# State-space layer with a gated feed-forward block on one core: the first token block's normalization, its high and low halves, the first feed-forward products, and the stores at the end

## The chip, the cores and the metric

The kernel runs on one NeuronCore of a Trainium2 chip, as one program. The metric is the device time of one execution in microseconds (us), the median of the runs; lower is better. Engines are named as in the profile: PE is TensorE (matmuls; PEld its weight loads), DVE is VectorE, ACT is ScalarE, POOL is GpSimd and SP is SyncE, which here only issues DMAs.

## What is computed

The input is 2048 tokens of 640 channels, in float32. The reference, cut to what matters:

```python
mod = (silu(c) @ w_mod)                      # six rows: sa, ca, ga, sb, cb, gb
h = layernorm(x) * (1 + ca) + sa
x = x + ga * (causal_conv(h, K) + h * D_skip)   # K: length 2048, from 128 complex states per channel
h = layernorm(x) * (1 + cb) + sb
x = x + gb * ((silu(h @ w1) * (h @ w3)) @ w2)   # w1, w3: 640 x 1728, w2: 1728 x 640
```

The convolution goes by a long transform in the reference; the kernel makes the same transform out of matmuls. The change touches none of that stage but one instruction of its layer norm. It touches the second half: the second layer norm, the gated feed-forward layer (FFN), and the final output.

## The kernel before

**Front.** Up to about 352 us of the profile the kernel makes the convolution's filters, the first layer norm, the transforms and the products in the frequency domain. These tasks are placed by a planner from a fixed list. At the end of it the inverse transform gives the convolved rows back, 128 tokens by 640 channels at a time ("slots"; 16 slots, four to a block of 512 tokens; blocks b = 0 to 3). The last 128 columns of block 0's four slots come last: `inverse_load` fetches the rows (tile `low`) and `inverse` multiplies them into PSUM tiles `iy` (lines 1234 and 1236). The inverse of the other three blocks is spread in pieces between the FFN's tiles of blocks 0 and 1.

**Second layer norm, block 0** (`ln2`, line 645, with `ln_norm`, 629, and `rsqrt`, 246). DVE sums the statistics, and `rsqrt` makes 1/sqrt(variance) for 4 values a partition with 13 small DVE instructions, each of which needs the one before: a start value from the bits of the float (a shift and a multiply-add on integers), three Newton steps of three instructions, and one for the shift -mean/sqrt(variance). Then the four slots are normalized into `xn` (slots 0 and 2 on ACT, 1 and 3 on DVE), turned by PE into PSUM banks `tp00` to `tp04` (one for each 128 channels k, 512 tokens wide; tags acc0 to acc4, which the FFN later sums in), scaled and shifted into `v` (even k on DVE, odd k on ACT), rounded by ACT into the high half `xh`, and the rest is subtracted out as the low half `xl` (even k on DVE, odd k on POOL; `split`, 625). While PE has nothing to do, `awake` gives it products that nobody reads.

**FFN** (`ffn`, 764). The hidden width of 1728 is 13 f-tiles of 128 and an odd one of 64, number 13, whose two 64-wide halves (w1 and w3) share a tile. The order is 0, 13, 1, 2, ... 12. `up` (1043) sums for an f-tile two PSUM tiles `gu` (w1 and w3; the odd tile one) over k = 0 to 4, with three matmuls for each k: wh times xh, wh times xl, wl times xh, where wh and wl are the high and low halves of the weights. The `gu` tiles have three PSUM banks. For block 0 the first two f-tiles' three sums are made together: 45 matmuls. `gate` (1056) makes `th` on ACT, then `a` on DVE in two steps, and its halves; `down` (1080) multiplies by w2 into `acc0` to `acc4`. Blocks 2 and 3 go by a scheme that shares products between the pair (`pair_up`, `pair_down`).

**End.** For block 3 the last f-tile is 12, and the one before is 11. `acc0` to `acc3` hold the output of the four slots for channels 0 to 511; `acc4` holds channels 512 to 639 turned, so `turn_last` (1896) copies it out on ACT (`oc`) and turns it by PE into `to`. `output` (1090) adds the residual `x` on DVE and stores two slots at once, 160 KB for each of four groups of 32 partitions. SP and ACT issue these stores in turn.

**What sets the order.** A scheduler places the instructions of the second half by priority; where the code uses `Engines`, `InOrder` (138, 156) or `order`, the written order is kept. Every DMA that SP or ACT issues takes the next of eight semaphores in turn (DMAHW0 to DMAHW7), and waits, before it is issued, until the DMA that used that semaphore before has landed. An engine does its instructions strictly in order, DMA issues among them.

Of the kernel before, what the change touches and what calls it, by code (L numbers as in the profile page):

```python
# [210 lines left out]
class K:  # L211
# [34 lines left out]
    def rsqrt(self, pool, var, n, tag, mean, scale=1.0, work=None):  # L246
# [347 lines left out]
    def inverse(self, j0, nj, z, ps, tag, bufs, d0, d1, part=None):  # L594
# [4 lines left out]
        for o, n in cuts if part is None else cuts[part:part + 1]:  # L599
            for j in range(0, nj, 2):  # L600
                py = [ps.tile([P, 512], F32, name=f"iy{j0 + j + p}_{d0 + o}", tag=tag, bufs=bufs) if ps else self.pbank(f"iy{j0 + j + p}") for p in range(2)]
                for p in range(2):
                    for q in range(4):
                        r, c = 64 * ((q + p) % 2), 32 * q
                        mm = nc.tensor.matmul(py[p][c:c + 32, :n], self.wd[r:r + 64, j0 + j + p, q // 2],
                                              z[q // 2][r:r + 64, j + p, o:o + n], start=True, stop=True, tile_position=(r, c))
# [22 lines left out]
    def ln_norm(self, b, pool, stats=None):  # L629
# [8 lines left out]
        for j in range(4):  # L638
            if j % 2:
                nc.vector.tensor_scalar(xn[:, j, :], xs[:, j, :], rstd[:, j:j + 1], nb[:, j:j + 1], op0=ALU.mult, op1=ALU.add)  # L640
            else:
                nc.scalar.activation(xn[:, j, :], xs[:, j, :], AF.Identity, scale=rstd[:, j:j + 1], bias=nb[:, j:j + 1])
        return xn

    def ln2(self, b, pool, ps, stats=None, po=None):
# [5 lines left out]
        xl = to.tile([P, KT, 512], F32R, name=f"xl{b}", tag="xl", bufs=1)  # L651
        for k in range(KT):
            if po:
                pt = po.tile([P, 512], F32, name=f"tp{b}{k}", tag=f"acc{k}")
            else:
                pt = ps.tile([P, 512], F32, name=f"tp{b}{k}", tag="gu", bufs=3)
            for j in range(4):
                nc.tensor.transpose(pt[:, j * P:(j + 1) * P], xn[:, j, k * P:(k + 1) * P], self.ident)
            v = pool.tile([P, 512], F32, name=f"v{b}{k}", tag="v", bufs=4)
            if po and k % 2:  # L660
                nc.scalar.activation(v, pt, AF.Identity, scale=self.cols[:, 1, k:k + 1], bias=self.cols[:, 0, k:k + 1])
            else:
                nc.vector.tensor_scalar(v, pt, self.cols[:, 1, k:k + 1], self.cols[:, 0, k:k + 1], op0=ALU.mult, op1=ALU.add)
            self.split(xh[:, k, :], xl[:, k, :], v, nc.gpsimd if po and k % 2 else nc.vector)
# [283 lines left out]
    def pair_down(self, wp, pool, ps, po):  # L948
# [20 lines left out]
        for b in (2, 3):  # L969
            acc = None  # L970
            for m in order:
# [14 lines left out]
                if pend is not None:  # L986
                    self.down(*pend, *([(4, 0, 1, 2)] if end else []))
# [55 lines left out]
    def up(self, b, tiles, xh, xl, ps):  # L1043
# [4 lines left out]
        for ks in [(k,) for k in range(KT)] if len(tiles) > 1 else [range(KT)]:  # L1048
            for pg, wh, wl in every:
                for k in ks:  # L1050
                    nc.tensor.matmul(pg, wh[:, k, :], xh[:, k, :], start=(k == 0), stop=False)  # L1051
                    nc.tensor.matmul(pg, wh[:, k, :], xl[:, k, :], start=False, stop=False)  # L1052
                    nc.tensor.matmul(pg, wl[:, k, :], xh[:, k, :], start=False, stop=(k == KT - 1))  # L1053
# [62 lines left out]
    def run(self):  # L1116
# [119 lines left out]
        self.hold = nc.tensor.prev = self.inverse(0, 4, z, ps, "gu", 3, cut, D)  # L1236
# [719 lines left out]
```

## Time and profile before

| what | value |
|---|---|
| runs | 931.13, 931.5, 933.71 us; median 931.5 us |
| profiled execution, own time | 932.87 us |
| its span in the trace | 931.1 us, so 1.77 us lie around the span |
| mean granted TensorE clock | 0.984 |
| DVE, ACT, POOL busy | 74%, 56%, 38% of the span |
| block 0, from the last inverse rows to the FFN | 352 to 375 us |
| FFN of all blocks | 365 to 924 us |

The profile's page gives the busy time of each engine, and the chain of work that ended last. The views used below are the waits of one engine (who it waited for, how long), the timeline of a window (start, length, engine, line, what is written and read, and in brackets the idle time before it and who ended it), the windows (busy time of each engine in a stretch), and the DMAs of a window (size, and microseconds from issue to landing). "x5" is the number of instructions joined in a row, and the length is then that of all of them.

### The profile page before, as it was taken

To read this page: it belongs to the slowest core of one execution; us is meant where nothing else is said; L and a number is where in the kernel's file an instruction comes from. 1 tells how busy PE (TensorE), PEld (TensorE's weight loads), DVE (VectorE), ACT (ScalarE), POOL (GpSimd) and SP (SyncE) were. 2 spreads that over 40 slices of the span, in tenths; PEclk is the share of its full clock that TensorE was granted. 3 is DMA by queue.
4 is the path that set the end of the run, shared out by engine and by line. 5 is a ranking of instruction groups with operands and counts; after the bars stand their busy time and mean duration, and the time that the engine had idled before them with its cause. 6 is when DMAs were issued, how large, how long until landed. Compare 5 with 4: busy or idle time off the path is not lost.

```text
span 931.1 us, 22000 instructions
## 1 busy us (share of the span) xinstructions
PE 846.5 (91%) x8983; PEld 678.7 (73%) x8983; DVE 692.1 (74%) x1213; ACT 519.2 (56%) x889; POOL 354.2 (38%) x341
## 2 busy tenths in 40 slices
PE   1367888999989997999999999999999999999997
PEld 1155767778868754777877788888888888888885
DVE  7999999999989776656765756476567777765653
ACT  5989999999877733423423334344333444445331
POOL 1589989899998461000000000001133332101640
PEclk9978999999999998999999999999999999999999
DMA  8965574332242568975455362232232111123242
GB/s 194 305 223 148 174 188 107 94 110 78 70 126 80 145 170 208 218 195 149 117 128 127 92 178 85 84 87 84 71 85 57 56 56 39 35 84 114 85 142 57
DMA packets 124556, 112.77 MB, mean 121 GB/s; under 512 B 11944, under 2 KB 106664, under 8 KB 123176
## 3 DMA queue, kind: packets, MB, share of 16 engines
q1 hardware_dynamic: 123720, 110.46, 43.6%
q8 instruction: 70, 1.15, 0.5%
q10 hardware_dynamic: 736, 0.92, 0.4%
q14 instruction: 30, 0.25, 0.1%
HBM read 90.38 MB, written 20.97 MB: 120 GB/s over the span
## 4 chain that ended last, share of the span: by engine, by line
PE 71%; DVE 11%; ACT 8%; DMA 4%; issue 3%; SPq 1%; POOL 0%; DVEq 0%; ACTq 0%; POOLq 0%
PE acc L1088 20%; PE p L837 17%; PE gu L1051 7%; PE gu L1053 7%; PE gu L1052 7%; PE ps L147 3%; DVE yy L147 3%; PE kps L147 2%; PE fh L147 2%; PE fz L147 2%; ACT tr L147 2%; PE fk L147 1%; DVE fp L147 1%; DVE xx L147 1%; DMA xs<-in_x 1%
## 5 line engine op out<-in xcount | busy, mean ns | idle before, releaser
L1051 PE MATMUL gu<-xh,wh 128*128 128x512 f32 x270 | 106.1, 398 | 1.6 <-ACT xh L626 1.4
L1053 PE MATMUL gu<-xh,wl 128*128 128x512 f32 x270 | 105.4, 390 | 0.0
L1052 PE MATMUL gu<-xl,wh 128*128 128x512 f32 x270 | 105.1, 389 | 0.0
L147 ACT ACTIVATE tr<-ph 128x512 f32<-128x512 int32 (+1 forms) x160 | 93.6, 602 | 8.9 <-POOL ph L147 3.0
L856 POOL TENSOR_TENSOR ws<-wp 128x256 f32<-128x256 f32 x13 | 9.6, 741 | 230.9 <-DVE x L627 116.0
L147 POOL TENSOR_TENSOR ph<-p,p 128x1024 int32<-128x1024 int32 x40 | 79.1, 1978 | 5.9 <-ACT tr L147 4.9
L147 DVE TENSOR_TENSOR yy<-yy,tr 128x512 f32<-128x512 f32 (+1 forms) x80 | 75.4, 943 | 1.4 <-POOL yy L147 1.2
L740 ACT ACTIVATE wh<-wr 128x640 fp32r<-128x640 f32 x51 | 34.9, 731 | 61.8 <-PE gu L1052 61.1
L837 PE MATMUL p<-x,wch 128*128 128x512 f32 x208 | 68.3, 389 | 0.0
L1051 PEld LDWEIGHTS gu<-xh,wh 128*128 128x128 f32 x270 | 50.6, 188 | 17.6 <-DVE al L627 2.1
L147 POOL TENSOR_TENSOR yy<-e,e 128x512 f32<-128x512 f32 x48 | 51.6, 1087 | 23.4 <-ACT e L147 19.7
L753 POOL MEMSET w2l<- 64x640 f32 x1 | 0.6, 632 | 157.0 <-PE acc L1088 157.0
L147 PE MATMUL kps<-yy,xx 128*32 128x64 f32 x2560 | 49.0, 227 | 11.5 <-DVE xx L147 9.1
L1053 PEld LDWEIGHTS gu<-xh,wl 128*128 128x128 f32 x270 | 50.7, 188 | 11.2 <-DVE wl L750 0.4
L1052 PEld LDWEIGHTS gu<-xl,wh 128*128 128x128 f32 x270 | 50.7, 188 | 10.2 <-DVE xl L627 0.2
L147 DVE TENSOR_TENSOR xx<-tr,xx 128x512 f32<-128x512 f32 x80 | 54.2, 680 | 2.2 <-ACT tr L147 1.7
L874 DVE TENSOR_TENSOR s<-p,s 128x512 f32<-128x512 f32 x52 | 34.7, 682 | 26.8 <-ACT s L872 22.8
L1064 ACT ACTIVATE th<-gu 128x512 f32<-128x512 f32 x26 | 15.5, 598 | 68.1 <-PE gu L1053 68.1
L1066 DVE TENSOR_TENSOR a<-a,gu 128x512 f32<-128x512 f32 x26 | 17.8, 686 | 46.6 <-PE gu L1053 46.4
L147 PEld LDWEIGHTS kps<-yy,xx 128*32 128x32 f32 x2560 | 43.2, 113 | 12.3 <-POOL yy L147 4.7
L147 PE MATMUL ps<-wk,xb 128*64 128x128 f32 x640 | 47.6, 295 | 2.9 <-issue 1.2
L147 PE MATMUL fh<-sp,wb 128*64 128x128 f32 x640 | 43.9, 280 | 5.7 <-issue 2.3
(381 smaller groups left out, 2386.5 us busy)
## 6 DMA issues: line engine op xcount, KB each, us to landing
wr<-in_w SPq DMA_DIRECT2D x52, 320.0 KB, 3.7
zd<-zt SPq DMA_DIRECT2D x39, 256.0 KB, 3.6
w2r<-in_w SPq DMA_DIRECT2D x26, 320.0 KB, 2.9
wp<-in_w SPq DMA_DIRECT2D x26, 320.0 KB, 3.2
wq<-in_w SPq DMA_DIRECT2D x26, 320.0 KB, 3.1
low<-zd SPq DMA_DIRECT2D x24, 320.0 KB, 6.3
xs<-in_x SPq DMA_DIRECT2D x16, 320.0 KB, 11.9
hs<-hb SPq DMA_DIRECT2D x20, 256.0 KB, 3.7
```

What stands on the lines that cost most here:

```text
L147: self.prev = self.k.order(f(*a, **kw), self.prev)
L740: self.nc.scalar.activation(wh[:, i], raw[:, i], AF.Copy)
L753: self.nc.gpsimd.memset(w2l[64:].bitcast(F32), 0.0)
L837: nc.tensor.matmul(to, t[:, o], y[:, k], start=start and k == i == 0, stop=stop and (k, i) == (n - 1, 2), skip_group_check=True)
L856: G.tensor_tensor(s[0], a21, a22, op=ALU.add)
L874: add = lambda o, bk, s: V.tensor_tensor(o, bk, s, op=ALU.add)
L1051: nc.tensor.matmul(pg, wh[:, k, :], xh[:, k, :], start=(k == 0), stop=False)
L1052: nc.tensor.matmul(pg, wh[:, k, :], xl[:, k, :], start=False, stop=False)
L1053: nc.tensor.matmul(pg, wl[:, k, :], xh[:, k, :], start=False, stop=(k == KT - 1))
L1064: nc.scalar.activation(th, gu[0], AF.Tanh, scale=0.5)
L1066: nc.vector.tensor_mul(a, a, gu[1])
L1088: nc.tensor.matmul(acc[k], *two(a, w), start=(m == 0 and i == 0), stop=(m == 12 and i == 2))
```

## The change

Six edits, all in the second half but for one instruction:

1. `rsqrt`: the two integer instructions become one (a multiply by -0.5 and an add). Where no work tile is given (all second layer norms), three Newton steps are replaced by one step of third order and one Newton step: 10 DVE instructions where there were 13. The first layer norm has a work tile, and loses one instruction.
2. `inverse` of block 0's last columns: PSUM tiles acc0 to acc3 instead of the three `gu` banks.
3. `ln_norm`, block 0: slot 2 is shared, columns 0 to 383 on ACT and 384 to 639 on DVE.
4. `ln2`, block 0: the turns stand in a fixed order, all four slots of a k together, slots 1, 0, 3, 2. `xh` is made by ACT straight from PSUM. Then `v` and `xl` for k = 0, 1, 2, 4 are made on DVE in turn, each k complete before the next; for k = 3 `v` on ACT after the last `xh`, and `xl` on POOL.
5. `up`, block 0, first two f-tiles: the two sums of f-tile 0 first, with the xl products of a k one step later than its other products, then the odd tile's 15 matmuls. 45 matmuls as before.
6. End: the three matmuls of f-tile 11 into acc2 stand behind `turn_last`; the residual is added for acc0, acc1, the last 128 channels (all four slots at once), acc2, acc3 in turn, and each of the five is stored by itself in four DMAs of 64 KB: 20 DMAs where there were 8 of 160 KB.

```diff
@@ rsqrt
-        nc.vector.tensor_scalar(wi, v.bitcast(I32), 1, None, op0=ALU.logical_shift_right)
-        nc.vector.tensor_scalar(wi, wi, -1.0, float(0x5F3759DF), op0=ALU.mult, op1=ALU.add)
-        for i in range(3):
...
+        nc.vector.tensor_scalar(wi, v.bitcast(I32), -0.5, float(0x5F3759DF), op0=ALU.mult, op1=ALU.add)
+        if work:
...
+        else:
+            nc.vector.tensor_mul(t, w, w)
+            nc.vector.tensor_mul(t, t, v)
+            nc.vector.scalar_tensor_tensor(t, t, -10.0 / 3.0, t, op0=ALU.add, op1=ALU.mult)
+            nc.vector.scalar_tensor_tensor(w, t, 5.0, w, op0=ALU.add, op1=ALU.mult)
+            nc.vector.tensor_mul(t, w, w)
+            nc.vector.scalar_tensor_tensor(t, t, -0.5 * 0.375 ** 3, v, op0=ALU.mult, op1=ALU.mult)
+            nc.vector.scalar_tensor_tensor(y, t, 1.5 * 0.375, w, op0=ALU.add, op1=ALU.mult)
@@ ln_norm
+            if stats and j == 2:
+                shared = 384
+                nc.scalar.activation(xn[:, j, :shared], xs[:, j, :shared], AF.Identity, scale=rstd[:, j:j + 1], bias=nb[:, j:j + 1])
...
+        if stats:
+            nc.vector.tensor_scalar(xn[:, 2, shared:], xs[:, 2, shared:], rstd[:, 2:3], nb[:, 2:3], op0=ALU.mult, op1=ALU.add)
@@ ln2
+            if po:
+                for j in (1, 0, 3, 2):
+                    last = self.order(nc.tensor.transpose(pt[:, j * P:(j + 1) * P], xn[:, j, k * P:(k + 1) * P], self.ident), last)
+                high.append(nc.scalar.activation(xh[:, k, :], pt, AF.Identity, scale=self.cols[:, 1, k:k + 1], bias=self.cols[:, 0, k:k + 1]))
+                todo.append((v, pt, k))
+                continue
...
+        for v, pt, k in todo:
+            scale, shift = self.cols[:, 1, k:k + 1], self.cols[:, 0, k:k + 1]
+            if k == 3:
+                self.order(nc.scalar.activation(v, pt, AF.Identity, scale=scale, bias=shift), high[-1])
+            else:
+                before = self.order(nc.vector.tensor_scalar(v, pt, scale, shift, op0=ALU.mult, op1=ALU.add), before)
+            i = (nc.gpsimd if k == 3 else nc.vector).tensor_tensor(xl[:, k, :], v, xh[:, k, :].bitcast(F32), op=ALU.subtract)
+            before = before if k == 3 else self.order(i, before)
@@ end of pair_down
-                    self.down(*pend, *([(4, 0, 1, 2)] if end else []))
+                    self.down(*pend, *([(4, 0, 1)] if end else []))
...
-        self.down(*pend, (2,))
-        self.down(*prev, (3,))
-        self.down(*pend, (3,))
-        self.output(3, acc, ps, pt)
+        for k in (2, 3):
+            self.down(*prev, (k,))
+            self.down(*pend, (k,))
+        x = self.x2[3]
+
+        def store(j, s):
+            for q in range(4):
+                (nc.scalar if q % 2 else nc.sync).dma_start(self.ov[q, :, 12 + j.start:12 + j.stop, s], x[q * 32:(q + 1) * 32, j, s])
+        for j in range(4):
+            nc.vector.tensor_add(x[:, j, :512], acc[j], x[:, j, :512])
+            store(slice(j, j + 1), slice(0, 512))
+            if j == 1:
+                nc.vector.tensor_add(x[:, :, 512:], pt, x[:, :, 512:])
+                store(slice(0, 4), slice(512, D))
@@ up
+            for k in range(KT + 1):
+                for w, x, c in ((1, xh, k), (2, xh, k), (1, xl, k - 1)):
+                    for t in every[:2] if 0 <= c < KT else ():
+                        last = self.order(nc.tensor.matmul(t[0], t[w][:, c, :], x[:, c, :], start=(c == 0 and w == 1 and x is xh), stop=(x is xl and c == KT - 1)), last)
+            every = every[2:]
...
@@ run
-        self.hold = nc.tensor.prev = self.inverse(0, 4, z, ps, "gu", 3, cut, D)
+        self.hold = nc.tensor.prev = self.inverse(0, 4, z, po, "acc", 0, cut, D)
```

The order of the built program at three places. A row names the line, the operation, the tile written, the tiles read and the shape; "waits" names the engines or DMA semaphores that the instruction waits for. First PE in block 0, from the turns to the first sums (gu0_00 and gu0_01 are f-tile 0's two sums, gu0_130 the odd tile's), before:

```order
L658 MATMUL tp00_5618<-ident_58,xn0_5611 128x128 x2
L658 MATMUL tp01_5627<-ident_58,xn0_5611 128x128 x2
...
L658 MATMUL tp04_5654<-ident_58,xn0_5611 128x128 x2
L1051 MATMUL gu0_00_5667<-xh0_5616,wh0_0_5413 128x512
L1051 MATMUL gu0_01_5668<-xh0_5616,wh0_0_5413 128x512
L1051 MATMUL gu0_130_5669<-xh0_5616,wh0_13_5495 128x512
L1052 MATMUL gu0_00_5667<-xl0_5617,wh0_0_5413 128x512
L1053 MATMUL gu0_00_5667<-xh0_5616,wl0_0_5440 128x512
```

and of the changed kernel:

```order
L674 MATMUL tp00_5615<-ident_58,xn0_5607 128x128 x4
L674 MATMUL tp01_5622<-ident_58,xn0_5607 128x128 x4
...
L674 MATMUL tp04_5643<-ident_58,xn0_5607 128x128 x4
L1089 MATMUL gu0_00_5664<-xh0_5613,wh0_0_5412 128x512
L1089 MATMUL gu0_01_5665<-xh0_5613,wh0_0_5412 128x512
L1089 MATMUL gu0_00_5664<-xh0_5613,wl0_0_5439 128x512
L1089 MATMUL gu0_01_5665<-xh0_5613,wl0_0_5439 128x512
...
L1089 MATMUL gu0_00_5664<-xl0_5614,wh0_0_5412 128x512
L1089 MATMUL gu0_01_5665<-xl0_5614,wh0_0_5412 128x512
```

Before, PE made two slots' turns for all five k and then the other two slots', and the first xl product was the fourth product. Now a k is turned completely before the next, the first xl product is the ninth, and the odd tile's products stand behind all 30 of f-tile 0. Next DVE at the same place, before:

```order
L640 TENSOR_SCALAR xn0_5611<-x_low_4178,rs_y_n0_5595,rs_n_n0_5596 128x640
L663 TENSOR_SCALAR v00_5623<-tp00_5618,cols_67 128x512 [waits PE_49]
L663 TENSOR_SCALAR v02_5641<-tp02_5636,cols_67 128x512 [waits PE_49]
L627 TENSOR_TENSOR xl0_5617<-v00_5623,xh0_5616 128x512 [waits Activation_49]
L663 TENSOR_SCALAR v04_5659<-tp04_5654,cols_67 128x512 [waits DVE_49,PE_49]
L627 TENSOR_TENSOR xl0_5617<-v02_5641,xh0_5616 128x512 [waits Activation_49]
L627 TENSOR_TENSOR xl0_5617<-v04_5659,xh0_5616 128x512 [waits Activation_49]
```

and of the changed kernel:

```order
L650 TENSOR_SCALAR xn0_5607<-x_low_4177,rs_y_n0_5594,rs_n_n0_5595 128x640
L654 TENSOR_SCALAR xn0_5607<-x_low_4177,rs_y_n0_5594,rs_n_n0_5595 128x256
L687 TENSOR_SCALAR v00_5616<-tp00_5615,cols_67 128x512 [waits Activation_49]
L688 TENSOR_TENSOR xl0_5614<-v00_5616,xh0_5613 128x512 [waits DVE_49]
L687 TENSOR_SCALAR v01_5623<-tp01_5622,cols_67 128x512 [waits Activation_49]
L688 TENSOR_TENSOR xl0_5614<-v01_5623,xh0_5613 128x512 [waits DVE_49]
L687 TENSOR_SCALAR v02_5630<-tp02_5629,cols_67 128x512 [waits Activation_49]
L688 TENSOR_TENSOR xl0_5614<-v02_5630,xh0_5613 128x512 [waits DVE_49]
```

Before, a `v` on DVE waited for PE's turns, and ACT's `xh` read it. Now `v` waits for ACT, which reads the same bank for `xh` first, and nothing but `xl` reads it. Last, the stores on SP at the end of the program (ACT issues as many, in turn with SP), before, behind the last weight loads:

```order
L963 DMA wq1_9440<-in_w2 128x640 [waits DMAHW3_49,DVE_49]
L147 DMA out_0<-x23_5544 32x1280 [waits DMAHW5_49,DVE_49]
L147 DMA out_0<-x23_5544 32x1280 [waits DMAHW6_49]
L147 DMA out_0<-x23_5544 32x1280 [waits DMAHW1_49,DVE_49]
L147 DMA out_0<-x23_5544 32x1280 [waits DMAHW2_49]
```

and of the changed kernel:

```order
L988 DMA wq1_9428<-in_w2 128x640 [waits DMAHW3_49,DVE_49]
L147 DMA out_0<-x23_5543 32x512 [waits DMAHW5_49,DVE_49]
L147 DMA out_0<-x23_5543 32x512 [waits DMAHW6_49]
L147 DMA out_0<-x23_5543 32x512 [waits DMAHW0_49,DVE_49]
L147 DMA out_0<-x23_5543 32x512 [waits DMAHW2_49]
L147 DMA out_0<-x23_5543 32x4x128 [waits DMAHW4_49,DVE_49]
L147 DMA out_0<-x23_5543 32x4x128 [waits DMAHW6_49]
L147 DMA out_0<-x23_5543 32x512 [waits DMAHW0_49,DVE_49]
L147 DMA out_0<-x23_5543 32x512 [waits DMAHW2_49]
L147 DMA out_0<-x23_5543 32x512 [waits DMAHW4_49,DVE_49]
L147 DMA out_0<-x23_5543 32x512 [waits DMAHW6_49]
```

With 8 stores each had a semaphore of its own, so what its first wait names is an older DMA. With 20 stores the third set of four (the last 128 channels, 32x4x128) takes the semaphores of the first set (acc0), the fourth (acc2) those of the second (acc1), and the fifth (acc3) those of the third.

One more place differs: on SP the load of w2's rows for f-tile 2 moves behind the next eight loads of `x` and four of `low`. The other differences of the order are a row or two wide.

More of the change, by code (lines that the diff above doesn't have):

```diff
@@ L254, in rsqrt @@
         wi = w.bitcast(I32)
-        nc.vector.tensor_scalar(wi, v.bitcast(I32), 1, None, op0=ALU.logical_shift_right)
-        nc.vector.tensor_scalar(wi, wi, -1.0, float(0x5F3759DF), op0=ALU.mult, op1=ALU.add)
-        for i in range(3):
-            if work:
+        nc.vector.tensor_scalar(wi, v.bitcast(I32), -0.5, float(0x5F3759DF), op0=ALU.mult, op1=ALU.add)
+        if work:
+            for i in range(3):
                 nc.vector.tensor_copy(u, w)
-            nc.vector.tensor_mul(t, u, w)
-            nc.vector.scalar_tensor_tensor(t, t, -0.5, v, op0=ALU.mult, op1=ALU.mult)
-            nc.vector.scalar_tensor_tensor(y if i == 2 else w, t, 1.5, w, op0=ALU.add, op1=ALU.mult)
+                nc.vector.tensor_mul(t, u, w)
+                nc.vector.scalar_tensor_tensor(t, t, -0.5, v, op0=ALU.mult, op1=ALU.mult)
+                nc.vector.scalar_tensor_tensor(y if i == 2 else w, t, 1.5, w, op0=ALU.add, op1=ALU.mult)
+        else:
[6 more added lines that the diff above has]
+            nc.vector.scalar_tensor_tensor(y, t, 1.5 * 0.375, w, op0=ALU.add, op1=ALU.mult)
         m, s = mean
@@ L600, in inverse @@
             for j in range(0, nj, 2):
-                py = [ps.tile([P, 512], F32, name=f"iy{j0 + j + p}_{d0 + o}", tag=tag, bufs=bufs) if ps else self.pbank(f"iy{j0 + j + p}") for p in range(2)]
+                py = [ps.tile([P, 512], F32, name=f"iy{j0 + j + p}_{d0 + o}", **(dict(tag=tag, bufs=bufs) if bufs else dict(tag=f"{tag}{j + p}"))) if ps else self.pbank(f"iy{j0 + j + p}") for p in range(2)]
                 for p in range(2):
@@ L638, in ln_norm @@
         for j in range(4):
-            if j % 2:
+            if stats and j == 2:
+                shared = 384
+                nc.scalar.activation(xn[:, j, :shared], xs[:, j, :shared], AF.Identity, scale=rstd[:, j:j + 1], bias=nb[:, j:j + 1])
+            elif j % 2:
                 nc.vector.tensor_scalar(xn[:, j, :], xs[:, j, :], rstd[:, j:j + 1], nb[:, j:j + 1], op0=ALU.mult, op1=ALU.add)
@@ L651, in ln2 @@
         xl = to.tile([P, KT, 512], F32R, name=f"xl{b}", tag="xl", bufs=1)
+        last = before = None
+        todo, high = [], []
         for k in range(KT):
@@ L1047, in up @@
         every = [(pg, wh[:, i], wl[:, i]) for (m, wh, wl), g in zip(tiles, gu) for i, pg in enumerate(g)]
[L1048 to L1053, printed above, removed]
+        last = None
+        if len(tiles) > 1:
+            for k in range(KT + 1):
[3 more added lines that the diff above has]
+            every = every[2:]
+        for pg, wh, wl in every:
+            for k in range(KT):
+                for w, x in ((wh, xh), (wh, xl), (wl, xh)):
+                    mm = nc.tensor.matmul(pg, w[:, k, :], x[:, k, :], start=(k == 0 and x is xh and w is wh), stop=(k == KT - 1 and w is wl))
+                    if len(tiles) > 1:
+                        last = self.order(mm, last)
         return gu
```

8 lines of the change are left out of this document (3 added, 5 removed).

## The prediction

> **What bounds the kernel now.** I read the page first, for the share of the chain of work that ended last, then PE's waits, then the two places of the change in the timeline, then the DMAs of the end.
>
> ```profile
> span 931.1 us, 22000 instructions
> PE 71%; DVE 11%; ACT 8%; DMA 4%; issue 3%; SPq 1%; POOL 0%; DVEq 0%; ACTq 0%; POOLq 0%
> ```
>
> The chain lies on PE for 71%. How firmly, the windows say (length, then PE, PEld, DVE, ACT, POOL busy, granted clock, DMA share, GB/s): two in the FFN, and two at block 0's start.
>
> ```profile
> 358.00:360.00 2.00, 2.00 (x4) 0.57 (x2) 1.61 (x10) 0.00 (x0) 0.00 (x0) 0.69 1.01 315
> 360.00:362.00 2.00, 1.23 (x10) 1.01 (x10) 1.13 (x2) 1.73 (x2) 0.00 (x0) 1.00 1.03 309
> 450.00:500.00 50.00, 49.92 (x271) 39.63 (x270) 32.91 (x72) 18.16 (x29) 0.00 (x0) 1.00 0.45 113
> 660.00:720.00 60.00, 60.00 (x267) 49.26 (x266) 42.58 (x60) 22.20 (x35) 17.81 (x20) 1.00 0.29 77
> ```
>
> From 375 to 925 us, PE's list of waits has one row:
>
> ```profile
> PE gu L1051 <- DVE a L1065: 0.2, 1, 0.2
> ```
>
> So between block 0's first products and the end PE is a solid row of matmuls. Time taken out ahead of it moves the whole row forward; time taken from other engines inside it (the shorter root of blocks 1 to 3 among it) is worth nothing. Only two places can gain: the hole before the first products, and the end, where PE is done and the stores land.
>
> **Block 0.** The timeline from the root to the next f-tile (start, length, engine, line, tiles):
>
> ```profile
> 356.59 3.63 PE L147 MATMUL awake<-x_low,ident 128*128 128x512 f32 x5
> 357.38 0.17 DVE L253 TENSOR_SCALAR rs_v_n<-mv_n 128x4 f32<-128x4 f32 x1
> 359.76 0.16 DVE L265 SCALAR_TENSOR_TENSOR rs_n_n<-mv_n,rs_y_n 128x4 f32<-128x4 f32 x1
> 360.01 1.73 ACT L642 ACTIVATE xn<-x_low,rs_n_n,rs_y_n 128x640 f32<-128x640 f32 x2 [12.94 <-DVE rs_n_n L265]
> 360.03 1.13 DVE L640 TENSOR_SCALAR xn<-x_low,rs_y_n,rs_n_n 128x640 f32<-128x640 f32 x2
> 360.99 2.40 PE L658 MATMUL tp<-ident,xn 128*128 128x128 f32 x20 [0.77 <-ACT xn L642]
> 362.56 1.53 DVE L663 TENSOR_SCALAR v<-tp,cols 128x512 f32<-128x512 f32 x2 [1.40 <-PE tp L658]
> 362.77 1.45 ACT L661 ACTIVATE v<-tp,cols 128x512 f32<-128x512 f32 x2 [1.03 <-PE tp L658]
> 364.12 2.93 ACT L626 ACTIVATE xh<-v 128x512 fp32r<-128x512 f32 x5
> 364.79 0.97 PE L1051 MATMUL gu<-xh,wh 128*128 128x512 f32 x3 [1.40 <-ACT xh L626]
> 365.40 3.00 POOL L627 TENSOR_TENSOR xl<-v,xh 128x512 fp32r<-128x512 f32 x2 [15.03 <-ACT xh L626]
> 373.14 0.39 PE L1051 MATMUL gu<-xh,wh 128*128 128x512 f32 x1
> 374.95 0.39 PE L1053 MATMUL gu<-xh,wl 128*128 128x512 f32 x1
> 374.01 0.60 ACT L1064 ACTIVATE th<-gu 128x512 f32<-128x512 f32 x1 [5.67 <-PE gu L1053]
> 375.55 0.47 PE L1051 MATMUL gu<-xh,wh 128*128 128x512 f32 x1 [0.21 <-DVE a L1065]
> 376.53 0.40 PE L1051 MATMUL gu<-xh,wh 128*128 128x512 f32 x1
> ```
>
> *Root.* From the first of 13 instructions (357.38) to the last (359.76) are 12 steps in 2.38 us, 0.198 each; three fewer are 0.6 us. ACT's first `xn` starts at 359.4 instead of 360.01. The awake products end at 360.22 (356.59 + 3.63), before the first turn, which needs an `xn` of 0.87 (half of 1.73) and so comes at 360.3. The clock is granted in full from 360 on in the second window, so the earlier turns meet it.
>
> *To the first product.* Before, 4.78 us pass from ACT's first `xn` to the product at 364.79: both slots on ACT, turns, `v`, `xh`. After, the slot that ends last is slot 2: ACT needs 0.87 and then 384 columns, an estimate of 0.6 (`th`, 512 columns, took 0.60; a 640-column `xn` 0.87), so 1.45 us; DVE has its 256 columns by then too (1.13 for two slots, 0.3 more). Of the 20 turns three stand before slot 2's first; 17 follow at 0.11 to 0.12 (2.40 for 20), 1.9 us. With 0.07 for the handover the first product starts 3.42 us after ACT's first `xn`. `xh` of k = 0 is no later: its turns end at 1.8, and an eviction by ACT takes 0.7 to 0.8 (1.45 for two), so 2.6. First product: 359.41 + 3.42 = **362.8, 2.0 us earlier**.
>
> *The 45 products.* Eight steps from 373.14 to 374.95 are 0.226 us each; 45 are 10.2, and before they took 375.55 - 364.79 = 10.76, the rest being starts of k that waited. After, f-tile 0's sums are complete at product 30, so `th`, `a` and the next weights' halves have the odd tile's 3.4 us to be made in, and the next f-tile starts without a wait at 373.0. Its first three products also run at 0.68 rather than 0.98 (375.55 to 376.53). Gains 0.5 and 0.3. Sum of block 0: **2.8**.
>
> *What it costs.* `v` on DVE now queues behind ACT's `xh`, and each pair of `v` and `xl` is a DVE chain; a late `xl` holds PE's row. DVE needs 0.8 for `v` (1.53 for two), and for `xl`:
>
> ```profile
> L627 DVE TENSOR_TENSOR xl<-v,xh x13: 677/684/1771, 364.8 to 572.5; 128x512 fp32r<-128x512 f32 x13
> ```
>
> 0.69, but 1.77 at worst, which in this block fell while POOL made its two `xl`. Counted from ACT's first `xn`: `xl` of k = 0, 1, 2, 4 at 4.2, 5.8, 7.3, 8.9; PE wants them at 5.2, 6.6, 8.0, 9.8 (products 9, 15, 21 and 29). POOL's one `xl` of 1.5 (3.00 for two) starts behind ACT's sixth eviction at about 6.2 and is done at 7.8, wanted at 9.3. It meets DVE's third `xl`; a stretch by 1.1 makes a stall of 0.4, a full block of 1.5 one of 0.85. I take 0.2: **block 0 gains 2.6**, with ends 1.6 (0.85 of stall, 0.2 for a slower 384-column piece, 0.15 for handovers) and 3.0 (PSUM banks for all four slots spare the statistics a wait).
>
> The Trainium skill, page "SBUF — State Buffer", section "SBUF: two separate sides", says that a DVE instruction with two SBUF inputs and a GpSimd instruction that reads SBUF lock each other out for a whole instruction. The 1.77 beside 0.68 agrees with it; by that rule the stall is the 0.85 above if POOL comes first, and the whole change is worth 0.65 less.
>
> Behind it, the shift must not run into data. PE's next rows of the inverse need `low`, loaded late because each DMA waits for the landing of the one eight issues before it:
>
> ```profile
> 365.85 4.96 SPq L589 DMA_DIRECT2D low<-zd  x4
> x<-in_x SPq DMA_DIRECT2D x1, 320.0 KB, 7.4
> low<-zd SPq DMA_DIRECT2D x4, 320.0 KB, 11.7
> L605 PE MATMUL iy<-low,x_low x16: 429/441/453, 386.2 to 389.7; 64*32 64x320 f32 x16
> ```
>
> The x load of 358.43 landed after 7.4, at 365.83, and only then `low` was issued; the last of the four (370.3) landed at about 382, and its reader ran at 386.2. Moved forward 2.6 it runs at 383.6: 1.5 us are left, and `low` gets a 320 KB load less ahead of it.
>
> **First layer norm.** One instruction less:
>
> ```profile
> 57.07 0.23 DVE L147 TENSOR_SCALAR rs_w_h<-rs_w_h 128x16 int32<-128x16 int32 x1
> ```
>
> DVE is full there; I take 0.1, between 0 and 0.25.
>
> **The end.**
>
> ```profile
> 920.99 1.38 DVE L147 TENSOR_TENSOR x<-acc,x 128x512 f32<-128x512 f32 x2 [2.15 <-PE acc L147]
> 924.20 0.69 DVE L147 TENSOR_TENSOR x<-acc,x 128x512 f32<-128x512 f32 x1 [0.70 <-PE acc L147]
> 924.80 0.41 DVE L147 TENSOR_TENSOR x<-to,x 128x256 f32<-128x256 f32 x1
> 925.25 0.87 ACTq L147 DMA_DIRECT2D out<-x  x2
> out<-x ACTq DMA_DIRECT2D x1, 160.0 KB, 3.0
> out<-x ACTq DMA_DIRECT2D x2, 160.0 KB, 4.0
> sp<-in_x SPq DMA_DIRECT2D x12, 64.0 KB, 2.0
> DMA to landing us min/median/max: 2.3/4.4/12.1
> ```
>
> The last add ends at 925.21, two stores on each queue are issued 0.43 apart, and the last (925.65) lands 4.0 later, at 929.65. After, the last add is acc3's and ends at 924.89 as before (PE does the same matmuls), so 0.36 is gained at the issue; but the fifth set waits for the third's landing, and that for the first's. Acc0's sum is ready 0.68 earlier (three matmuls moved behind it), its add runs from 920.3 to 921.0, the second store of a queue goes at 921.5, and with L from issue to landing the end is 921.5 + 3L. **Break-even is L = 2.7.** L of a 64 KB store isn't in the trace. Below stand the 64 KB loads (2.0) and the fastest DMA on `zd` (2.3, of 256 KB or more); above, a 160 KB store at 3.0 with three others beside it, and 4.0 in the last set. A set of four now moves 256 KB, not 640, so I go by the low rows: L = 2.3, end 928.4, **gain 1.2**; ends: 2.1 gained (L = 2.0), 0.9 lost (L = 3.0).
>
> The Trainium skill, page "DMA: Bandwidth & Descriptors", section "Anatomy of one DMA — SWDGE (gpsimd) path", gives about 2.0 us fixed plus bytes by 436 GB/s, an estimate of 2.15 for 64 KB and 2.4 for 160 KB, and would have the end at 927.95, a gain of 1.7. The trace's 3.0 and 4.0 for 160 KB lie above it, so I don't go by it; its "Rules for kernel authors" ask for few large transfers, which speaks for the next rival but one.
>
> **Sum.** 2.6 + 0.1 + 1.2 = 3.9 us. The profiled execution took 932.87 (span 931.1 and 1.77 around it), so it would take 929.0; the median of the runs shown is 931.5, 1.4 lower, so **927.6**.
>
> **Rivals.**
> - *The slots don't bind.* Landings of 2.0 as the 64 KB loads: the end gains 2.1, together 4.8, 926.7. Against it: the writes of 160 KB took 3.0 at best.
> - *The end gives nothing.* 20 issues and L of 2.7 to 3.0, as the first set's stores: 0 to 0.9 lost, 928.8 to 929.7. For it: more DMAs, half as large, and every set waits for a set.
> - *Slower.* Landings that don't shrink with size, at 4.0 like the last set's, three in a chain: the end is 933.5, 3.9 later, which takes back the 2.7 ahead of it: 932.7. It decides from L = 3.6 on. Against it: the 4.0 came with 640 KB in flight.
> - *Block 0's shift is caught by data.* `low` lands 1.5 to 2.7 later than now: PE waits and gives back up to 1.2: 928.8. For it: DMA share is 1.0 there; against: the load taken out ahead.
>
> **Chances.** Forecast 0.60 (926.8 to 928.6), slots not binding 0.12, end without gain 0.17, slower 0.05, shift caught 0.06. A measurement tells 0.3% (2.8 us) from no change: faster is below 928.7. That is the first two less a tail of 0.04: 0.68. Slower by over 0.3% needs L = 4.5: 0.03. Same 0.29. The range leaves out the slow case and the corners where all ends meet: 926.1 to 930.2.
>
> **What would show it.** First `gu` product near 362.8 and no PE wait for `xl` over 0.4; the next f-tile's first product near 373.0; no wait of PE for `low`; the stores' issues in the timeline spaced by landings of 2.0 to 2.6, acc3's add ending 2.7 earlier than 924.89, and the span's end 1.2 closer to it. Wrong would make me: landings over 2.7, or PE held by DVE's `xl`.

## The result and the profile after

The changed kernel took 926.84 us (median of 7 runs, 924.1 to 929.6), beside 931.41 us before (7 runs, 930.3 to 933.71): ratio 0.9943, 95% interval 0.9926 to 0.9959. Measured once more beside other runs of before it was 928.67 to 933.45, ratio 0.9951, interval 0.9934 to 0.9969. So it is faster by 4.6 and by 4.8 us at the medians, where 3.9 was forecast (927.6).

The first profile of it has a span of 922.3 us, 8.8 less than before's 931.1. Most of the difference from the forecast is in the front, and not of the change: PE's timelines, first of before and then of the changed kernel, agree to 0.01 us at 155 us.

```profile
154.58 2.06 PE L147 MATMUL fh<-sp,wb 128*64 128x128 f32 x32 [0.67 <-DVE fp L147]
```

```profile
154.57 2.06 PE L147 MATMUL fh<-sp,wb 128*64 128x128 f32 x32 [0.69 <-DVE fp L147]
```

In the next 15 us PE of before waits twice for nothing that the profile shows; these are two rows of its waits, and the changed kernel's list of that window has no such row:

```profile
PE ps L147 <- issue: 1.5, 1, 1.5
PE fh L147 <- issue: 1.0, 1, 1.0
```

The `ps` products behind these waits start at 167.46 in before and at 164.97 in the changed kernel, so that is 2.5 of the 4.2 us by which block 0's last inverse rows come earlier (348.57 for 352.81). In the fourteen profiles of this study these rows start anywhere from 348.6 to 356.4 us. So the front is left out below: each part is measured from an event just ahead of it.

Block 0 in the timeline of the changed kernel, to be laid beside the forecast's first long list:

```profile
353.12 0.17 DVE L253 TENSOR_SCALAR rs_v_n<-mv_n 128x4 f32<-128x4 f32 x1
354.90 0.16 DVE L272 SCALAR_TENSOR_TENSOR rs_n_n<-mv_n,rs_y_n 128x4 f32<-128x4 f32 x1
355.17 0.92 ACT L652 ACTIVATE xn<-x_low,rs_n_n,rs_y_n 128x640 f32<-128x640 f32 x1 [11.73 <-DVE rs_n_n L272]
355.94 2.88 PE L674 MATMUL tp<-ident,xn 128*128 128x128 f32 x20 [0.94 <-DVE xn L650]
355.99 0.69 ACT L648 ACTIVATE xn<-x_low,rs_n_n,rs_y_n 128x384 f32<-128x384 f32 x1
357.15 3.45 ACT L675 ACTIVATE xh<-tp,cols 128x512 fp32r<-128x512 f32 x5 [0.47 <-issue]
358.57 0.71 PE L1089 MATMUL gu<-xh,wh 128*128 128x512 f32 x2
361.42 1.29 POOL L688 TENSOR_TENSOR xl<-v,xh 128x512 fp32r<-128x512 f32 x1 [14.70 <-ACT v L685]
361.71 1.55 DVE L688 TENSOR_TENSOR xl<-v,xh 128x512 fp32r<-128x512 f32 x1
363.31 0.30 PEld L1089 LDWEIGHTS gu<-xl,wh 128*128 128x128 f32 x2 [0.36 <-DVE xl L688]
369.11 0.39 PE L1094 MATMUL gu<-xh,wh 128*128 128x512 f32 x1
369.79 0.39 PE L1094 MATMUL gu<-xh,wh 128*128 128x512 f32 x1
```

From ACT's first `xn` to the first product are 3.40 us (358.57 - 355.17; 4.78 before), the 45 products take 10.54 (369.11 - 358.57; 10.76 before), the next three 0.68 (0.98 before). The turns start early and end just ahead of the first product: PE doesn't wait for `xh` any more. Within the 45 products it waits once, 0.36 us, for DVE's third `xl`.

The end of the changed kernel, timeline and DMAs of the window:

```profile
913.53 1.39 DVE L147 TENSOR_TENSOR x<-acc,x 128x512 f32<-128x512 f32 x2 [1.51 <-PE acc L147]
914.25 5.08 SPq L147 DMA_DIRECT2D out<-x  x10
917.43 0.69 DVE L147 TENSOR_TENSOR x<-acc,x 128x512 f32<-128x512 f32 x1 [0.69 <-PE acc L147]
...
out<-x SPq DMA_DIRECT2D x10, 64.0 KB, 2.1
out<-x ACTq DMA_DIRECT2D x10, 64.0 KB, 2.0
```

acc3's add ends at 918.12 and the span at 922.3, 4.2 us behind it; before it was 931.1 - 924.89 = 6.2. The stores start 3.9 us ahead of that point; before, 2.2. Between, the row of matmuls is as long as before: 547.2 us from the start of the next f-tile's fourth product to acc3's last in both (923.77 - 376.53, and 917.01 - 369.79). So between these two profiles the gain of the change is 2.5 in block 0, counted from the start of the last inverse rows, and 2.0 at the end.

The last inverse rows come in two groups, and PE waits for `low` ahead of each. Before, and then in the changed kernel:

```profile
352.81 0.63 PE L605 MATMUL iy<-low,x_low 64*32 64x128 f32 x2 [3.70 <-DMA low<-zd]
353.95 1.70 PE L605 MATMUL iy<-low,x_low 64*32 64x128 f32 x30 [0.51 <-DMA low<-zd]
```

```profile
348.57 0.40 PE L612 MATMUL iy<-low,x_low 64*32 64x128 f32 x2 [3.62 <-DMA low<-zd]
349.97 1.27 PE L612 MATMUL iy<-low,x_low 64*32 64x128 f32 x30 [1.00 <-DMA low<-zd]
```

The table gives these parts for all kernels run, in us. "To first": from the start of the last inverse rows (the product that ends PE's wait of some 3.6 us for `low`) to the first product; "45": from there to the next f-tile's first; "3": its first three products; "block 0": from the second group of the inverse rows (353.95 and 349.97 above) to the start of that f-tile's fourth product; "end": from acc3's add ending to the end of the span; "stores": from the first store's issue to the end of the span.

| kernel | inverse rows at | to first | 45 | 3 | block 0 | end | stores |
|---|---|---|---|---|---|---|---|
| before | 352.81 | 11.98 | 10.76 | 0.98 | 22.58 | 6.20 | 8.36 |
| changed | 348.57 | 10.00 | 10.55 | 0.68 | 19.83 | 4.17 | 8.05 |
| changed, again | 352.05 | 9.89 | 10.56 | 0.68 | 19.84 | 4.23 | 8.12 |
| new end alone | 353.44 | 12.21 | 10.73 | 0.98 | 22.56 | 4.03 | 7.92 |
| new block 0 alone | 352.68 | 9.85 | 10.54 | 0.68 | 19.82 | 6.26 | 8.43 |
| 12 stores | 352.23 | 9.89 | 10.55 | 0.68 | 19.83 | 5.37 | 7.95 |
| 16 stores | 352.35 | 10.00 | 10.53 | 0.68 | 19.81 | 4.99 | 8.18 |
| last channels by POOL | 352.72 | 9.91 | 10.53 | 0.68 | 19.82 | 4.16 | 8.04 |
| acc0 first, xl on DVE | 356.41 | 10.11 | 10.33 | 0.68 | 19.62 | 3.87 | 8.41 |
| xl on DVE | 353.37 | 10.04 | 10.31 | 0.68 | 19.59 | 4.22 | 8.09 |
| root of 13 | 350.61 | 10.46 | 10.54 | 0.68 | 20.42 | 4.12 | 7.99 |
| v first | 351.56 | 11.41 | 10.38 | 0.68 | 21.02 | 4.13 | 8.00 |
| sums k by k | 351.27 | 9.93 | 11.47 | 0.99 | 21.06 | 4.24 | 8.11 |
| gu banks, slot 2 whole | 351.47 | 10.37 | 10.55 | 0.68 | 20.19 | 4.21 | 8.09 |

"To first" holds the second wait for `low`, of 0.5 to 1.0 us, and scatters with it; "block 0" begins behind that wait and hardly scatters. It is 22.56 and 22.58 in the two kernels with the old block 0, and 19.81 to 19.84 in the six with the new one unedited: the new block 0 is worth 2.74 us. The end, unedited, is 4.03 to 4.24 in eight kernels.

Six kernels (16 stores, last channels by POOL, root of 13, v first, sums k by k, gu banks) were executed once, in 926.59 to 928.73 us. With a front that scatters by several us a single time places nothing, so only their parts are read.

### The profile page after: what moved, and what is told of

It is laid out like the page before. It is cut to its first block, busy times and chain, and to the rows that moved or that the text cites. A ratio compares the mean times of both kernels' runs of the same rounds, so it can differ in the third digit from the quotient of the medians.

```text
span 922.3 us, 22008 instructions
## 1 busy us (share of the span) xinstructions
PE 840.1 (91%) x8983; PEld 676.5 (73%) x8983; DVE 690.4 (75%) x1202; ACT 518.8 (56%) x888; POOL 352.3 (38%) x340
## 4 chain that ended last, share of the span: by engine, by line
PE 71%; DVE 12%; ACT 7%; DMA 5%; issue 3%; SPq 1%; DVEq 0%; ACTq 0%
PE acc L1131 20%; PE gu L1094 19%; PE p L862 17%; DVE yy L147 3%; PE ps L147 3%; PE fz L147 2%; DVE fp L147 2%; PE kps L147 2%; PE fh L147 2%; ACT tr L147 2%; DVE xx L147 2%; DMA xs<-in_x 1%; SPq L147 1%; PE fk L147 1%; ACT xs L147 1%
## 5 line engine op out<-in xcount | busy, mean ns | idle before, releaser
L1094 PE MATMUL gu<-xh,wh 128*128 128x512 f32 x260 | 103.3, 397 | 0.0
L1094 PE MATMUL gu<-xh,wl 128*128 128x512 f32 x260 | 101.4, 390 | 0.0
L1094 PE MATMUL gu<-xl,wh 128*128 128x512 f32 x260 | 101.3, 389 | 0.0
L1094 PEld LDWEIGHTS gu<-xh,wl 128*128 128x128 f32 x260 | 48.8, 188 | 10.5
L147 PEld LDWEIGHTS ps<-wk,xb 128*64 128x64 f32 x640 | 43.1, 219 | 7.0 <-issue 2.2
```

Source lines behind the costliest of these rows:

```text
L147: self.prev = self.k.order(f(*a, **kw), self.prev)
L1094: mm = nc.tensor.matmul(pg, w[:, k, :], x[:, k, :], start=(k == 0 and x is xh and w is wh), stop=(k == KT - 1 and w is wl))
```

## The experiments

### The two halves apart

The new end on the kernel before:

```diff
-                    self.down(*pend, *([(4, 0, 1, 2)] if end else []))
+                    self.down(*pend, *([(4, 0, 1)] if end else []))
...
-        self.down(*pend, (2,))
-        self.down(*prev, (3,))
-        self.down(*pend, (3,))
-        self.output(3, acc, ps, pt)
...
```

> The kernel before with the new end alone (acc2's three matmuls moved, five sets of 64 KB stores). Theory (two separate gains, and a front that differs from run to run): from acc3's add ending to the end of the span 4.2 us where before has 6.2 (931.1 - 924.89), as in the changed kernel (922.3 - 918.12 = 4.2); so 2.0 faster, and the last inverse rows to the next f-tile's first product unchanged at 21.6 us. Rival (the end gives nothing by itself, the profiled run was only a lucky front): 6 us as before, no gain.

Measured: 931.07 beside 932.85 us, ratio 0.9978 (0.9965 to 0.9992); end 4.03, block 0 as before. The text above counts the 21.6 from the second group of inverse rows; so counted it is 21.58 here and 21.60 in before. By its part the new end is worth 2.2 us without the rest.

The changed kernel with the end of before (the same edit backwards):

> The changed kernel with the end of before (8 stores of 160 KB). Theory: the last inverse rows to the next f-tile's first product take 19.1 us (before 21.6), the third product of that f-tile another 0.3 less, the end 6.2 as before: 2.8 faster than before. Rival (the shorter root of the first layer norm, or the moved load, makes the front of 349 us some 3 to 4 us faster, which the profiled run of the changed kernel shows): 6 to 7 us faster, with the last inverse rows at about 349 in place of 353.

Measured: 931.24 beside 932.85 us, ratio 0.9980 (0.9964 to 0.9996), that is 0.4 to 3.4 us; inverse rows at 352.68, from there to the next f-tile 20.39 (22.74 before), from their second group 19.14, as expected, end 6.26. By its parts the gain is 2.74; the times are too coarse to place it closer. The two halves give 1.8 and 1.6 us at the medians, 3.4 together, where the whole gave 4.6 and 4.8; with intervals of 1.3 to 1.5 us to either side of each that is no contradiction. The inverse rows come where before has them, so the 348.57 was not the change's.

The changed kernel, unedited, again:

> The changed kernel once more, beside the runs of before on this chip, for its front. Theory: the 8.8 us between the two profiled spans are 4.5 of the change and 4.2 of a front that differs from run to run; last inverse rows at 350 to 354 us, block 0 and end as in the first profile, median 4 to 5 below before. Rival (the front's 4.2 belongs to the change): last inverse rows again near 348.6, and a median 7 to 9 below before.

Measured: ratio 0.9951 (0.9934 to 0.9969), 4.8 us at the medians; inverse rows at 352.05; the span is 925.8. The rival, a front of 4 us that belongs to the change, is out.

### What sets the end

Twelve stores in three sets:

```diff
         for j in range(4):
             nc.vector.tensor_add(x[:, j, :512], acc[j], x[:, j, :512])
-            store(slice(j, j + 1), slice(0, 512))
             if j == 1:
                 nc.vector.tensor_add(x[:, :, 512:], pt, x[:, :, 512:])
-                store(slice(0, 4), slice(512, D))
+                store(slice(0, 2), slice(0, D))
+            elif j > 1:
+                store(slice(j, j + 1), slice(0, D))
```

> The changed kernel with 12 stores in three sets: slots 0 and 1 together (160 KB each) behind acc1's add and that of the last 128 channels, then slot 2 and slot 3 (80 KB each). Theory (what is gained at the end is the small last set, and the semaphores cost a little): the last set takes the semaphores of the first set, which land before acc3's add is done, so its issue follows the add at once: acc3's add to the end of the span 3.8 to 4.1 us (4.2 in the changed kernel, where the last set's issue came 0.3 to 0.5 late). Rival (each slot has to go by itself early for the queue to be empty at the end): 4.6 or more.

Timeline and DMAs of that end:

```profile
919.15 4.76 SPq L147 DMA_DIRECT2D out<-x  x6
921.05 0.69 DVE L147 TENSOR_TENSOR x<-acc,x 128x512 f32<-128x512 f32 x1 [0.69 <-PE acc L147]
...
out<-x SPq DMA_DIRECT2D x4, 80.0 KB, 3.2
out<-x ACTq DMA_DIRECT2D x4, 80.0 KB, 3.8
```

Measured: end 5.37 (927.1 - 921.74), as the rival has it. But the last set didn't go at once behind acc3's add, as the theory had assumed. On SP its two stores were issued at 922.33 and 923.59, 0.6 and 1.85 behind the end of the add: the issue ahead of them lasted 1.30 us, and the second one waited 0.9 for a landing, in one piece, where the changed kernel waits 0.7 in three:

```profile
SPq L147 <- DMA out<-x: 0.9, 1, 0.9
```

So this run doesn't take the semaphores out. It shows that landings grow with what is queued: 80 KB took 3.2 (SP) and 3.8 (ACT) at the median, behind 640 KB, where 64 KB had taken 2.0. The first store comes 2.6 us ahead of acc3's add ending, in the changed kernel 3.9. From the first issue to the end both have 8 us (7.95 and 8.05), and so has before (8.36). That made the next theory: the 1.31 MB need their time from the first store on. The rows of DMA activity (a digit is a fortieth of a window of 10.1 and 10.0 us, in tenths of what 16 DMA engines can be busy) have 22 digits with work in both kernels, 5.5 us, without a hole; first before, then the changed kernel:

```profile
DMA  0000000000995969499965988787975100000000
```

```profile
DMA  0000000000087997979688899897798940000000
```

In all fourteen profiles the first byte moves 0.85 us behind the first issue, the bytes flow for 5.3 to 5.8 us, and 1.6 to 2.0 us pass from the last byte to the end of the span. In time: 929.8 beside 932.85 us, ratio 0.9958 (0.9943 to 0.9973).

Sixteen stores, acc0's waiting for acc1's add:

```diff
-            store(slice(j, j + 1), slice(0, 512))
+            if j:
+                store(slice(0 if j == 1 else j, j + 1), slice(0, 512))
```

> The changed kernel with 16 stores in four sets: acc0's and acc1's 512 columns together (128 KB each) behind acc1's add, then the last 128 channels, acc2, acc3 singly. Theory now, after the 12 stores (the queue is full from the first store on, so the end is the first issue plus the time for 1.31 MB): first issue 0.7 later, 3.2 before acc3's add ends in place of 3.9; acc3's add to the end of the span 4.7 to 5.0 us (4.2 in the changed kernel). Rival (the semaphores set it, as I forecast): the chain is of two landings in place of three, the last set goes at once behind its add, 3.8 to 4.0.

Measured: end 4.99, as the new theory has it; the chain of semaphores, one link shorter, gave nothing. By itself this doesn't rule the semaphores out either: the 128 KB stores took 2.8 us to land on ACT and the 64 KB ones behind them 3.1 to 3.4, and the last set, waiting for those, was issued 1.0 to 1.6 behind the add's end (921.95).

The last 128 channels issued by POOL:

```diff
-                (nc.scalar if q % 2 else nc.sync).dma_start(
+                (nc.gpsimd if s.start else nc.scalar if q % 2 else nc.sync).dma_start(
```

> The changed kernel with the four stores of the last 128 channels issued by POOL, which has semaphores of its own: 16 stores are left on SP and ACT, so acc3's set waits for acc1's landing in place of that of the last 128 channels. Theory (full queue from the first issue on): 4.1 to 4.4 us from acc3's add to the end of the span, as in the changed kernel. Rival (semaphores): 3.8 to 4.0.

The last issues of ACT in it, by size and time to landing, beside its add:

```profile
921.52 0.69 DVE L147 TENSOR_TENSOR x<-acc,x 128x512 f32<-128x512 f32 x1 [0.69 <-PE acc L147]
...
out<-x ACTq DMA_DIRECT2D x2, 64.0 KB, 2.6
```

Measured: end 4.16, the same as the changed kernel, and 0.16 outside the rival's 3.8 to 4.0, where the unedited end scatters from 4.03 to 4.24. This is the only one of the three in which the last set waits for no semaphore. The program's order names acc1's stores for it, and its stores are issued at 922.24 to 922.66, right behind the add (ends 922.21). In the changed kernel the last store goes 0.9 behind the add. Each of the set's issues is 0.3 to 0.5 nearer to the add than there. But they take 2.5 to 2.6 to land instead of 2.0. What was waited for at the issue is waited for in the queue.

acc0's sum finished first, with all `xl` on DVE (next experiment):

```diff
-        self.down(*pend, (4, 0, 1))
+        self.down(*pend, (0, 4, 1))
+        self.down(*prev, (2,))
         pt = self.turn_last(3, acc, ps)
-        for k in (2, 3):
-            self.down(*prev, (k,))
-            self.down(*pend, (k,))
+        self.down(*pend, (2,))
+        self.down(*prev, (3,))
+        self.down(*pend, (3,))
```

> The changed kernel with all five xl on DVE, and with the last f-tile's three matmuls into acc0 ahead of those into acc4, and f-tile 11's into acc2 ahead of the turns. Theory (a full queue from the first store on): the first store is issued 4.5 us before acc3's add ends (3.9 in the changed kernel), so the end is 3.5 to 3.8 us behind it (4.2); with the 0.2 of xl on DVE 0.6 to 0.9 faster than the changed kernel. Rival (the last set's own way sets the end: 0.4 of issue and 2.0 of landing behind the wait for a semaphore): 4.1 to 4.2, no gain at the end.

Its timeline:

```profile
921.32 5.35 SPq L147 DMA_DIRECT2D out<-x  x10
925.17 0.69 DVE L147 TENSOR_TENSOR x<-acc,x 128x512 f32<-128x512 f32 x1 [0.70 <-PE acc L147]
```

Measured: first store 4.54 ahead of the add's end, end 3.87, just outside the 3.5 to 3.8 expected: half of the 0.67 moved is gained. Now the last set goes at once (925.89, the add ends at 925.86) and lands in 2.1, as a store does with little ahead of it. What remains is the set's own way, 0.45 to its last issue (926.32), 2.1 of landing and about 1.3 to the end of the span, so the rival's floor was real, though lower than it had it. By its parts it is 0.5 us faster than the changed kernel (0.3 at the end, 0.2 in the 45 products). In time it can't be told from it: 928.26, ratio 0.9951 (0.9934 to 0.9968), with a front at 356.41 in its profile.

### What sets block 0

All five `xl` on DVE:

```diff
-            i = (nc.gpsimd if k == 3 else nc.vector).tensor_tensor(xl[:, k, :], v, xh[:, k, :].bitcast(F32), op=ALU.subtract)
-            before = before if k == 3 else self.order(i, before)
+            before = self.order(nc.vector.tensor_tensor(xl[:, k, :], v, xh[:, k, :].bitcast(F32), op=ALU.subtract), before)
```

> The changed kernel with all five xl on DVE and none on POOL. Theory (POOL's subtraction stretches DVE's third xl from 0.69 to 1.55, and PE waits 0.36 for it): every xl 0.69, no wait of PE for xl, the next f-tile's first product 18.8 us after the last inverse rows (19.1 in the changed kernel), 0.3 faster. Rival (the chain on DVE is what is late, POOL relieves it): xl of k = 4 comes 0.7 later and PE waits for it by 0.3 or more, no gain.

DVE's third and fourth `xl` in its timeline:

```profile
366.55 1.30 DVE L688 TENSOR_TENSOR xl<-v,xh 128x512 fp32r<-128x512 f32 x2
```

Measured: two in 1.30, none stretched, no wait of PE for `xl`; the 45 products take 10.31 instead of 10.55, and from the second group of inverse rows, from which the text above counts, the next f-tile starts after 18.91 (19.15). The theory holds with 0.24. DVE has room for the fifth; POOL's help cost more than it gave. In time: 928.67 beside 932.85 us, ratio 0.9957 (0.9941 to 0.9973).

The root of 13 instructions in the second layer norms:

```diff
+            nc.vector.tensor_scalar(wi, v.bitcast(I32), 1, None, op0=ALU.logical_shift_right)
+            nc.vector.tensor_scalar(wi, wi, -1.0, float(0x5F3759DF), op0=ALU.mult, op1=ALU.add)
+        for i in range(3):
...
```

> The changed kernel with the 13-instruction root in the second layer norms. Theory: three DVE steps of 0.198 come back on the path, last inverse rows to the first product 10.6 us (10.0 in the changed kernel), to the next f-tile's first product 21.15 (20.55). Rival (the root is covered by the awake products or by data): no change.

```profile
355.03 0.17 DVE L253 TENSOR_SCALAR rs_v_n<-mv_n 128x4 f32<-128x4 f32 x1
357.41 0.16 DVE L267 SCALAR_TENSOR_TENSOR rs_n_n<-mv_n,rs_y_n 128x4 f32<-128x4 f32 x1
```

Measured: 2.38 from the first to the last instruction, where the changed kernel has 1.78 (353.12 to 354.90): 0.60 for three instructions. To the first product 10.46, 0.5 later, with the scatter of `low` in it; from the root's last instruction to the first product 3.66 in both kernels, and "block 0" 0.59 longer. The root is on the path in full.

The first 45 products k by k over three sums, as before:

```diff
-            for k in range(KT + 1):
...
+        for ks in [(k,) for k in range(KT)] if len(tiles) > 1 else [range(KT)]:
+            for pg, wh, wl in every:
...
```

> The changed kernel with the first two f-tiles' 45 products in the order of before (three sums, k by k, xl products right behind xh's). Theory: the fourth product waits 0.2 to 0.4 for xl of k = 0, and the next f-tile's first products wait for the gate's work again: next f-tile's first product 0.4 to 0.8 later than in the changed kernel (20.55), the third another 0.3. Rival (the order is worth nothing): the same as the changed kernel within 0.1.

```profile
372.67 0.47 PE L1086 MATMUL gu<-xh,wh 128*128 128x512 f32 x1 [0.67 <-DVE a L1100]
```

Measured: 11.47 for the 45, 0.92 more, and 0.99 for the next three. The largest piece is the wait of 0.67 for `a`: all three sums end together, and the next f-tile finds neither a free bank nor its weights' halves (its weight loads wait 1.06 for `wh` and 0.38 for `wl`). So the order is worth 1.2, more than the 0.7 to 1.1 expected.

`v` first, `xh` out of it, as before:

```diff
-                for j in (1, 0, 3, 2):
...
+            if po and k % 2:
+                nc.scalar.activation(v, pt, AF.Identity, scale=self.cols[:, 1, k:k + 1], bias=self.cols[:, 0, k:k + 1])
...
+            self.split(xh[:, k, :], xl[:, k, :], v, nc.gpsimd if po and k % 2 else nc.vector)
```

> The changed kernel with the loop of the second layer norm as before: v first (even k on DVE, odd on ACT), then xh out of v, xl of odd k on POOL, turns in the scheduler's order. Theory (xh straight from PSUM takes an eviction off the path to the first product): last inverse rows to the first product 10.4 to 10.9 us (10.0 in the changed kernel). Rival (turns of PE are what is late, as the changed kernel's first product comes 0.1 behind the last turn): 10.0.

```profile
362.97 0.74 PE L1076 MATMUL gu<-xh,wh 128*128 128x512 f32 x2 [1.40 <-ACT xh L633]
```

Measured: to the first product 11.41, 1.4 to 1.5 later, more than expected; PE stands idle for 1.40 behind the turns, as in before. The `xl` come with less delay then, and the 45 take 10.38; by "block 0" the net is 1.2.

The `gu` banks for the inverse and slot 2 whole on ACT:

```diff
-z, po, "acc", 0, cut, D)
+z, ps, "gu", 3, cut, D)
...
-            if stats and j == 2:
+            if False:
...
-        if stats:
+        if False:
```

> The changed kernel with the last columns' inverse in the three gu banks and slot 2 normalized by ACT alone, as before. Theory: ACT's second slot takes 0.83 in place of 0.69, so the turns and the first product come 0.1 to 0.3 later than in the changed kernel (3.4 us behind ACT's first xn); the banks are worth 0 to 0.2 ahead of the root. Rival (the banks or the shared slot carry most of block 0's gain): 0.6 or more.

Measured: from ACT's first `xn` to the first product 3.62 in place of 3.40: 0.2 for the shared slot. From the second group of inverse rows to the root 3.29, where all kernels with the new banks have 3.15 or 3.16: 0.14 for the banks. The two kernels with the old block 0 have 3.43; where the other 0.14 come from wasn't tried. The four edits of block 0 that were taken back give 0.6, 1.2, 1.2 and 0.4, more than the 2.74 of the whole, so they share some of their gain.

## Why the prediction was right, and where it wasn't

**Block 0, forecast 2.6 (1.6 to 3.0), measured 2.74: right in its steps.** The root's 0.6: shown, 0.60. From ACT's first `xn` to the first product 3.42 forecast, 3.40 measured; the new bound named for it, the turns behind slot 2, is what the trace shows, since the first product follows the last turn by 0.03. Three products at 0.68: exact. The 45 products were put at 10.2 plus 0.2 and took 10.55: the stall beside POOL's `xl` was 0.36, at the place forecast (DVE's third `xl`), near the 0.4 that I had worked out and not the 0.2 that I took. POOL ran from 361.42 to 362.71, DVE's `xl` from 361.71 to 363.26, ending 0.55 behind POOL: it looks held for as long as POOL ran. The long `xl` of before (367.17 to 368.94, POOL to 368.39) ends 0.55 behind POOL too. Taking POOL away brought every `xl` to 0.69, which shows that POOL running beside it is the cause. The Trainium skill, page "SBUF — State Buffer", section "SBUF: two separate sides", has the loser of the shared port pair wait for the other's whole instruction; the trace agrees but for 0.14, since a whole `xl` takes 0.69 and this one ended 0.55 behind POOL. No run looks at the port itself. The term that the sum left at nothing is the PSUM banks: named for the upper end of the range only, they are worth 0.14, and 0.28 are gained ahead of the root in all.

**First layer norm, forecast 0.1: nothing to be seen.** DVE is 0.47 earlier behind that root, of which 0.25 are the root's and 0.22 were there ahead of it. But at 155 us PE is where it was, so it was lost in between; where isn't shown. One pair of profiles says so; it wasn't tried alone.

**The end, forecast 1.2 (-0.9 to 2.1): a gain of 2.0, by another mechanism.** The failed step is "the fifth set waits for the third's landing, and that for the first's", and the formula from it, 921.5 + 3L. The waits are there, the landings were 2.0 to 2.3, and the formula with 2.0 even gives the measured gain; that is the rival in which the slots don't bind, 2.1 by its numbers, and it had 0.12. But the runs show that the chain is not the reason: with no wait for the last set (POOL's queue) the end was the same. One link less (16 stores) ended 0.8 later, but there the last set still waited, so that run agrees with both accounts. What counts is when the first store goes, since the bytes then flow almost without a hole for their 5.3 to 5.8 us. The change brings it from 2.17 us ahead of acc3's add ending to 3.87 ahead, by 1.70, and the end came nearer by 2.0; the other 0.3 are the shorter stretch of stores, 8.05 for 8.36. From first issue to end of span all fourteen profiles have 7.9 to 8.4 us, with 8, 12, 16 or 20 stores. Of the moved first issue 0.68 are the matmuls into acc2 set behind, which I had, and 1.0 is acc0's store not waiting for acc1's and the last channels' adds, which I counted only as the chain's start. The small size of the stores, by which I chose between gain and loss, matters through this alone: a store of one slot can go when that slot is ready. So the gain forecast for the end came true by luck: its sum rested on a chain of landings that is not what sets the time.

The rival "slower" fell with its premise: 4.0 was no property of a store but of 640 KB in flight, as the argument against it had said. `low` was not late: from 370 us to the end PE's list of waits is empty in the changed kernel.

**The range and the sum.** 3.9 forecast, 4.57 at the medians. By the parts it is 2.74 and 2.0, 4.8 together, which is what the second set of runs has. The mis-sized term is the end, by 0.8. Block 0 was put 0.14 too low: the stall took 0.16 more than forecast, and the 0.28 ahead of the root weren't in the sum. The 0.1 of the first layer norm didn't come.

## What to carry to other kernels

At an end like this one, with 1.31 MB to store, count from the first store's issue: once the queue is full, neither fewer, larger stores nor a last set free of semaphores brought the end nearer, while finishing one accumulator early and storing it by itself did, until the last store finds little ahead of it. In this chain of small dependent instructions every one was on the path at its full 0.2 us, and an operand that the next engine needs first (here the high half) is worth making straight from PSUM, with the rest behind it. Helping a busy DVE with POOL on operands in SBUF can cost more than the help, when both run at the same time.

## What the runs showed of the hardware

- A 64 KB store lands 2.0 us after its issue with little ahead of it, 2.5 to 2.6 with several sets in flight (last channels by POOL), and 3.1 to 3.4 right behind 512 KB (16 stores); an 80 KB store in 3.2 and 3.8 at the median behind 640 KB (12 stores). The Trainium skill, page "DMA: Bandwidth & Descriptors", section "Anatomy of one DMA — SWDGE (gpsimd) path", has a fit for single DMAs that GpSimd issues, a fixed part plus bytes. By it an estimate is 2.15 for 64 KB and 2.2 for 80 KB: the first is near the 2.0, the second lies far below the 3.2 and 3.8, which hold the queue's time.
- The stores' bytes flow at some 240 GB/s: 1.31 MB in about 5.5 us of the changed kernel's end, with the DMA engines 0.86 busy, and in 5.3 to 5.8 us in all fourteen profiles. Why not faster wasn't tried.
- The DVE's `xl`, two operands in SBUF, took 1.55 us instead of 0.69 beside a POOL `xl` of 1.29, and 0.69 without it.
- One and the same program starts its last inverse rows 3.5 us apart in two profiles (348.57 and 352.05). In before's front some of PE's idle time ends with nothing that the profile shows; what it is stays open. This scatter is what made a change of 4.6 us need several runs, and why a single profiled span (8.8 us less) says little of it.
